# A block-sparse attention with an MLP behind it on one core: the heads of the values are loaded in another order

## The chip, the cores and the metric

The kernel runs on one core of a Trainium2 chip. The metric is the device time of one execution in microseconds (us). Five engines matter, each with its own queue: PE (TensorE, matrix products; its weight loads are listed as PEld), DVE (VectorE), ACT (ScalarE), POOL (GpSimd) and SP (SyncE). POOL and SP issue the transfers (DMAs), which 16 DMA engines carry out.

## The reference

`B, H, S, D = 4, 8, 768, 64`: four batches, eight heads, 768 tokens of 64 values. Attention is restricted to blocks of 32 tokens; its result, with the heads side by side, goes through an MLP with an exact GELU.

```python
scores = scale * np.matmul(q, k.transpose(0, 1, 3, 2))
# mask: neighbouring blocks, first and last block, 3 sampled blocks for each block
scores = np.where(mask, scores, -1000000000.0)
attn = softmax(scores)
x = np.matmul(attn, v)            # (B, H, S, D), then to (B*S, H*D) = (3072, 512)
h = x @ w_in                      # 512 -> 2048
out = gelu(h) @ w_out             # 2048 -> 512
```

## The kernel before

The work is cut into eight units: for each batch a dense one (tokens of three groups of 128, among them the first and the last block, which attend to everything) and one without dense blocks. The attention of unit n+1 runs with the second product of the MLP of unit n (`ffn2_pieces`) as filler between its steps; before it stands the first product of unit n's MLP (`ffn1_step`, L486), eight steps for each unit. The order on every engine is the order in which the program is written; nothing is moved by a scheduler.

Keys and values of a batch lie in one tile, `kvs[b % 2]`, so two batches are held at once. It has 128 partitions, 25 block positions and 388 columns for each: 128 columns of keys, then 260 of values. A head of the values is 24 blocks of 32 tokens with 64 values each. `load_v(b, h)` (L128 to L134) brings one head with one DMA that POOL issues: 32 partitions wide, 24 blocks, 64 values, from float32 in memory to bfloat16 in the tile, that is 768 pieces of 128 bytes written. The 32 partitions are one of four quarters, 0 to 3, and `hh ^= G` chooses it: heads 0 to 7 go to quarters 0, 1, 2, 3, 1, 0, 3, 2. Quarters 0 and 1 are partitions 0 to 63 (the lower half, L), quarters 2 and 3 are partitions 64 to 127 (the upper half, U). Two heads share a quarter's partitions and lie in different columns there, next to a column of ones each.

There are four such sets of eight loads, one for each batch:

- Batch 0, at the start: POOL issues the loads of the keys and queries (L102), the ones (L156), then the eight heads, then the parts of `w_in` (L139). The readers of the tile are the value products of the dense rounds (L400) on PE and POOL's copies of the sampled blocks into `gb` (`gather`, L277), which take all 128 partitions and all value columns.
- Batch 1, during the first product of unit 0's MLP by the program. `turn_keys` and `turn_queries(1)` are issued ahead of it, and `hold_loads` (L150), a tiny copy that reads `qT1`, makes POOL wait until the queries have been turned.
- Batches 2 and 3, each in the first product of an MLP, behind a `hold_loads` on `g`. POOL's copies for the next unit (L277) stand behind them.

The rounds of an attention go through `scores` (L316, PE), `maxima` (L341, L344, DVE), `exponentials` (L358, L362, ACT), `turned` (L375, L380, DVE), `values` (L400 and L436, PE; in pairs of half the heads each), `divided` (L451 to L455, DVE) and `outputs` (L465 on PE, L473 on ACT). `idle_products` (L518) are products without use that fill PE in the first attention.

Of the kernel before, what the change touches and what calls it, by code (L numbers as in the profile page):

```python
# [19 lines left out]
def kernel(  # L20
# [12 lines left out]
    B, H, S, D = q.shape  # L33
# [60 lines left out]
    def sampled(i, r):  # L94
        c0 = GW * (i // 3) + 4 * BW + DW * (i % 3) + BW * r
        return gb[:, c0:c0 + BW]

    def keys(b):
        return kvs[b % 2][:, :, 0:KC]
# [8 lines left out]
    def load_by_token(dst, src, b):  # L108
        rows = by_token(dst).rearrange("p (c h d) -> p c h d", h=H, d=D)
        for c in range(NC):  # L110
            nc.gpsimd.dma_start(out=rows[:, c],
                                in_=src[b, :, P * c:P * c + P].rearrange("h p d -> p h d"))
# [4 lines left out]
    def turn_keys():  # L117
        nc.sync.dma_start_transpose(out=kTd.rearrange("p (n s) -> p n s", s=P), in_=by_token(kn))

    def turn_queries(b):  # L120
        nc.sync.dma_start_transpose(out=qTs[b % 2].rearrange("p c r s -> p (c r) s"), in_=by_token(qn))
# [7 lines left out]
    def load_v(b, h):  # L129
        G, hh = divmod(h, 4)  # L130
        c0 = KC + V2 * G + VW * (hh % 2)
        hh ^= G
        nc.gpsimd.dma_start(out=kvs[b % 2][32 * hh:32 * hh + 32, 0:NB, c0:c0 + D],  # L133
                            in_=v[b, h].rearrange("(n p) d -> p n d", p=BL))  # L134

    def load_w_in(part, n=4):
        w = D_FF // n
        cols = slice(w * part, w * part + w)
        nc.gpsimd.dma_start(  # L139
            out=w_in_sb[:, :, cols], in_=moe_w_in[:, cols].rearrange("(ki p) f -> p ki f", p=P))  # L140
# [7 lines left out]
    def hold_loads(x):  # L148

        nc.gpsimd.tensor_copy(mark, x)  # L150

    def ones(i):
        for hh in range(4):
            for G in range(2):
                c0 = KC + V2 * G + VW * (hh % 2 ^ G) + D
                nc.gpsimd.memset(kvs[i][32 * hh:32 * hh + 32, 0:NB, c0:c0 + 1], 1.0)  # L156
# [18 lines left out]
    load_kq(qn, q, HALVES[0])  # L175
    load_kq(qn, q, HALVES[1])
    ones(0)
    for h in range(H):
        load_v(0, h)


    vf = const.tile([1, NB, NR], I32, name="vf")
# [64 lines left out]
    def gather_fixed(kT, place, copy=None, part=None):  # L247

        copy = copy or nc.vector.tensor_copy
        groups = gb.rearrange("p (g x) -> p g x", x=GW)  # L250
        js = sorted(place)
        runs = [[j for j in js if place[j] - j == c] for c in sorted({place[j] - j for j in js})]
        for run in runs if part != 1 else ():
            i0 = place[run[0]]
            assert i0 % 3 == 0
            for lane in range(min(3, len(run))):
                m, g0 = len(range(lane, len(run), 3)), i0 // 3
                c0, j = BW + KC * lane, run[0] + lane - 1
                copy(
                    groups[:, g0:g0 + m, c0:c0 + 3 * BW].rearrange("p g (w c) -> p g w c", c=BW)[:, :, :, 0:KC],  # L260
                    kT[:, j:j + 3 * m, :].rearrange("p (g w) c -> p g w c", w=3))
        if part == 0:
            return
        at = slice(min(place.values()) // 3, max(place.values()) // 3 + 1)
        n = at.stop - at.start
        copy(groups[:, at, 0:3 * KC].rearrange("p g (l c) -> p g l c", c=KC),
             kT[:, None, 0:1, :].to_broadcast([P, n, 3, KC]))
        copy(  # L268
            groups[:, at, 4 * BW:GW].rearrange("p g (l x) -> p g l x", x=DW)[:, :, :, NR * BW:DW],
            kT[:, None, NB - 1:NB, :].to_broadcast([P, n, 3, KC]))  # L270

    def gather(unit, js, at, c0=0, c1=BW, engine=None):

        src = k0 if (unit.b, c1) == (0, KC) else kvs[unit.b % 2][:, :, c0:c1]
        for j in js:
            for r in range(NR):
                (engine or nc.vector).tensor_copy(sampled(unit.place[j], r)[:, None, c0:c1],  # L277
                                                  src[:, bass.ds(at[j][r], 1), :])
# [105 lines left out]
    def table(func):  # L384

        nc.scalar.activation(junk, zero[0:1, 0:1], func)  # L386
# [94 lines left out]
    def ffn1_step(n, m):  # L481
        T = P * len(units[n].quads)
        hp = psA.tile([P, 2, 512], F32, name="hp", tag="A")
        for i in range(2):
            for ki in range(KIN):
                nc.tensor.matmul(hp[:, i, 0:T], lhsT=w_in_sb[:, ki, (m + i) * P:(m + i + 1) * P],  # L486
                                 rhs=xTs[n % 2][:, ki, 0:T], start=(ki == 0), stop=(ki == KIN - 1))
        for i in ((0, 2),) if m < KOUT - 2 else ((0, 1), (1, 2)):
            nc.scalar.activation(g[:, m + i[0]:m + i[1], 0:T], hp[:, i[0]:i[1], 0:T], AF.Gelu)  # L489
# [13 lines left out]
    def ffn2_pieces(n):  # L503
        for t, quad in enumerate(units[n].quads):
            store_finished()
            op = psO.tile([P, D_MODEL], F32, name="op")
            for m in range(KOUT):
                nc.tensor.matmul(op, lhsT=g[:, m, t * P:(t + 1) * P], rhs=w_out_sb[:, m, :],  # L508
                                 start=(m == 0), stop=(m == KOUT - 1))
                if m == KOUT - 1:  # L510
                    finished.append((n, quad, slice(0, D_MODEL), op))
                yield
# [145 lines left out]
    def more_numbers(js):  # L658
        def load():
            for c in range(0, len(js), 6):  # L660
                known.update(block_numbers(js[c:c + 6], DVE))
        return load
# [5 lines left out]
    def next_keys(b):  # L668
        place_keys(b)
        spare_key(keys(b))  # L670

    for n, unit in enumerate(units):
        nxt = units[n + 1] if n + 1 < len(units) else None
        b = unit.b
        fresh = nxt is not None and nxt.b != b
        if nxt is not None and not fresh:
            if n == 0:
                nc.vector.tensor_copy(kvs[0][:, :, 0:KC], k0)
                more_numbers(J1[6:8])()
            gather_fixed(keys(b), nxt.place)  # L680
            gather(nxt, J1[:8], known)
        for s in range(KOUT // 2):
            ffn1_step(n, 2 * s)
            if s == 0:
                if n == 0:
                    turn_keys()
                    turn_queries(1)
                    gather(nxt, J1[8:], others, engine=nc.gpsimd)
                    ones(1)
                    hold_loads(qT1[0:1, 0:1])  # L690
                    for h in range(H):
                        load_v(1, h)
                elif fresh and b + 2 < B:
                    xT, t0 = column[b, unit.groups[-2][0]]
                    hold_loads(xT[0:1, 0, t0:t0 + 1])
                    load_by_token(qn, q, b + 2)
                    load_by_token(kn, k, b + 2)
                    turn_queries(b + 2)
                elif nxt is not None and not fresh:
                    if b + 1 < B:  # L700
                        turn_keys()
                        hold_loads(g[0:1, 0, 0:1])
                        for h in range(H):
                            load_v(b + 1, h)
                    gather(nxt, J1[8:], others, engine=nc.gpsimd)
            if s == 7 and nxt is not None:
                table(AF.Exp)
                if n > 0 and not fresh and b + 1 < B:
                    next_keys(b + 1)
            if fresh and s == 0:  # L710
                gather_fixed(keys(b + 1), nxt.place)
                gather(nxt, J0[3:9], known)
                gather(nxt, J0[:3], known)
                hold_loads(sampled(nxt.place[J0[2]], NR - 1)[0:1, BW - 1:BW])
                gather(nxt, J0[9:], others, engine=nc.gpsimd)
        filler = ffn2_pieces(n)
        if nxt is None:
            last_output(n)
        elif fresh:
            attention(nxt, filler, [1, 7, 4, 3, 1, 5, 4, 7, 6], (2, 0, 6))  # L720
        elif b + 1 < B:
            attention(nxt, filler, [3, 11, 2, 5, 3, 8, 1, 7, 1], (5,), ahead=units[n + 2],
                      hooks={} if n else {
                          3: [lambda: next_keys(1)], 6: [more_numbers(J0[:3])]})
        else:
            attention(nxt, filler, [7, 6, 3, 5, 3, 8, 7], (1, 0, 5))
# [30 lines left out]
```

## Time and profile before

| | |
|---|---|
| runs of the kernel | 294.49, 298.87 and 293.29 us; median 294.49 us |
| profiled execution, its own time | 296.14 us |
| its span, first to last instruction | 294.4 us |
| mean granted TensorE clock | 0.983 of full |
| busy, share of the span | PE 89%, DVE 73%, ACT 69%, POOL 40% |
| DMAs issued by POOL (q0) | 68352 packets, 13.64 MB |
| instruction queue (q8) | 37 packets, 0.61 MB |
| loads of the values (L133) | 32 DMAs, 0.71 us of POOL's time each in the median |
| from issue to landing of such a load | 3.5 to 13.7 us, median 7.0 us |

The page cuts the span into 40 slices of 7.36 us. These two rows show the share of each slice, in tenths, in which PE was busy, and the clock it was granted:

```profile
PE   1667769978699999999999999999999999999994
...
PEclk9995999999799999999999999999999999999999
```

PE is at 9 tenths nearly everywhere from the twelfth slice on, but at 6 and 7 tenths in the first 50 us, and at 6 in the eleventh slice (74 to 81 us), where the clock was also lower for a part of the slice. The stretches between these times, and the loads in them, are what the change touches.

### The profile page before, as it was taken

Reading aid. Unit: us, or ns where it says so; the run is one execution under the profiler, and the core shown is the slowest. Engines: PE = TensorE matmul, PEld = TensorE weight load, DVE = VectorE, ACT = ScalarE, POOL = GpSimd, SP = SyncE. Lnnn points to the kernel's source line nnn. Section 1 sums busy time; section 2 is a strip of 40 time slices with the busy share of each in tenths; the row PEclk is TensorE's granted clock in tenths of the full one; section 3 lists DMA queues with packets and bytes.
Section 4 is the critical chain, followed back from the end, with each engine's and each line's share of the span. In section 5 each row is a group of like instructions: output and inputs, shape, how many; then the busy total and the mean of one; then the engine's idle time right before and its main releaser. Section 6 shows DMA issues by size and latency. Waiting matters only on the chain.

```text
span 294.4 us, 11255 instructions
## 1 busy us (share of the span) xinstructions
PE 262.4 (89%) x4793; PEld 142.5 (48%) x4793; DVE 213.5 (73%) x477; ACT 204.3 (69%) x374; POOL 118.8 (40%) x219
## 2 busy tenths in 40 slices
PE   1667769978699999999999999999999999999994
PEld 1523445534354455635553555445544555355644
DVE  7595839989697887688997969688948878782000
ACT  8776645686267875698668975796778756976621
POOL 8697999734098000970495005920040014000000
PEclk9995999999799999999999999999999999999999
DMA  6999999999499711991199218991100210021001
GB/s 105 159 86 193 191 166 156 160 172 89 43 115 156 94 73 45 145 72 70 13 154 170 65 40 129 101 61 40 40 0 2 75 39 2 3 74 38 2 36 72
DMA packets 90628, 25.36 MB, mean 86 GB/s; under 512 B 81745, under 2 KB 87634, under 8 KB 90578
## 3 DMA queue, kind: packets, MB, share of 16 engines
q0 software_dynamic: 68352, 13.64, 86.7%
q1 hardware_dynamic: 22226, 11.01, 16.5%
q8 instruction: 37, 0.61, 0.8%
q14 instruction: 13, 0.11, 0.1%
HBM read 27.26 MB, written 6.29 MB: 114 GB/s over the span
## 4 chain that ended last, share of the span: by engine, by line
PE 55%; ACT 17%; DMA 9%; DVE 6%; POOL 6%; issue 4%; POOLq 0%; DVEq 0%; ACTq 0%
PE hp L486 22%; PE op L508 16%; PE av L436 9%; ACT pp L358 8%; DMA kv<-in_v_dram 4%; ACT L386 4%; POOL gb L277 3%; DMA qn<-in_q_dram 3%; ACT g L489 2%; PE sc L316 2%; DVE nm L341 2%; DMA kn<-in_k_dram 2%; PE tx L465 2%; PE av L537 2%; PE op L537 2%
## 5 line engine op out<-in xcount | busy, mean ns | idle before, releaser
L508 PE MATMUL op<-w_out_sb,g 128*128 128x512 bf16 x336 | 87.2, 385 | 0.1
L486 PE MATMUL hp<-xT,w_in_sb 128*128 128x384 bf16 x512 | 85.0, 326 | 0.8 <-ACT xT L473 0.4
L358 ACT ACTIVATE pp<-sc,nm 128x256 bf16<-128x256 f32 x176 | 75.4, 545 | 13.7 <-DVE nm L341 13.5
L489 ACT ACTIVATE g<-hp 128x768 bf16<-128x768 f32 (+1 forms) x72 | 52.1, 738 | 31.4 <-PE hp L486 31.4
L486 PEld LDWEIGHTS <-w_in_sb 128*128 128x128 bf16 x512 | 49.9, 98 | 36.1 <-issue 3.1
L341 DVE TENSOR_REDUCE nm<-sc 128x4 f32<-128x1024 f32 (+1 forms) x48 | 52.9, 1108 | 5.2 <-PE sc L316 5.1
L277 POOL COPY gb<-kv 128x388 bf16 (+1 forms) x87 | 36.9, 475 | 26.4 <-DVE gb L268 24.1
L508 PEld LDWEIGHTS <-g 128*128 128x128 bf16 x336 | 28.8, 98 | 35.4 <-issue 11.9
L277 DVE COPY gb<-kv 128x388 bf16 x177 | 44.2, 329 | 0.5 <-DMA qn<-in_q_dram 0.5
L436 PEld LDWEIGHTS <-pT 64*32 64x32 bf16 (+1 forms) x2400 | 26.3, 92 | 24.0 <-DVE pT L375 10.8
L375 DVE STREAM_TRANSPOSE pT<-pp 128x512 f32<-128x512 f32 (+1 forms) x48 | 31.5, 656 | 4.5 <-ACT pp L358 4.3
L436 PE MATMUL av<-kv,pT 64*32 64x130 bf16 (+1 forms) x1344 | 28.0, 220 | 7.4 <-issue 4.8
L473 ACT COPY xT<-tx 128x512 bf16<-128x512 bf16 (+1 forms) x32 | 13.6, 450 | 20.6 <-PE tx L465 20.6
L316 PE MATMUL sc<-gb,qT 64*32 64x256 bf16 x704 | 19.2, 277 | 8.5 <-ACT pp L358 4.5
L150 POOL COPY mark<-g 1x1 bf16<-1x1 bf16 x2 | 7.0, 3500 | 43.7 <-ACT g L489 43.7
L133 POOL DMA_DIRECT2D kv<-in_v_dram x32 | 22.9, 725 | 1.8 <-DMA qn<-in_q_dram 1.7
L316 PEld LDWEIGHTS <-qT 64*32 64x32 bf16 x832 | 11.6, 90 | 23.8 <-issue 18.0
L362 ACT ACTIVATE pp<-sc,nm 128x768 bf16<-128x768 f32 x16 | 17.1, 1101 | 6.5 <-DVE nm L344 6.5
L344 DVE TENSOR_REDUCE nm<-sc 128x1 f32<-128x768 f32 x16 | 15.0, 945 | 8.4 <-PE sc L316 7.9
L436 PE MATMUL av<-gb,pT 64*32 64x130 bf16 x1056 | 19.9, 222 | 0.0
L386 ACT ACT_TABLE_LOAD x15 | 19.2, 1283 | 0.3
L451 DVE TENSOR_SCALAR den<-av 128x8 f32<-128x8 f32 (+2 forms) x28 | 4.6, 164 | 20.3 <-PE av L436 18.7
(73 smaller groups left out, 244.5 us busy)
## 6 DMA issues: line engine op xcount, KB each, us to landing
out_dram<-os SPq DMA_DIRECT2D x23, 256.0 KB, 2.1
kv<-in_v_dram POOLq DMA_DIRECT2D x32, 96.0 KB, 7.0
kn<-in_k_dram POOLq DMA_DIRECT2D x18, 128.0 KB, 5.4
qn<-in_q_dram POOLq DMA_DIRECT2D x18, 128.0 KB, 5.2
w_in_sb<-in_moe_w_in_dram POOLq DMA_DIRECT2D x4, 512.0 KB, 11.1
w_out_sb<-in_moe_w_out_dram POOLq DMA_DIRECT2D x4, 512.0 KB, 7.9
kn<-in_k_dram POOLq DMA_DIRECT2D x2, 384.0 KB, 5.2
qn<-in_q_dram POOLq DMA_DIRECT2D x2, 384.0 KB, 7.2
```

The lines of the kernel that those rows point to most:

```text
L133: nc.gpsimd.dma_start(out=kvs[b % 2][32 * hh:32 * hh + 32, 0:NB, c0:c0 + D], in_=v[b, h].rearrange("(n p) d -> p n d", p=BL))
L277: (engine or nc.vector).tensor_copy(sampled(unit.place[j], r)[:, None, c0:c1], src[:, bass.ds(at[j][r], 1), :])
L316: nc.tensor.matmul(o, lhsT=qT[rows, j // 4, pr, BL * (j % 4):BL * (j % 4) + BL], rhs=rhs(rows, pr), start=True, stop=True)
L341: nc.vector.tensor_reduce(out=nm[:, 0:2 * n].rearrange("p (g j) -> p g j", g=2), in_=A4[:, :, 0:n, :], op=ALU.max, axis=AX.X, negate=True)
L358: nc.scalar.activation(at[:, x // n, x % n], A[:, a:a + 256].rearrange("p (e c k) -> p e c k", e=2, k=BL), AF.Exp, bias=nm[:, x:x + 1])
L362: nc.scalar.activation(pp[:, 0:S].rearrange("p (c k e) -> p c e k", e=2, k=BL), A[:, 0:S].rearrange("p (c e k) -> p c e k", e=2, k=BL), AF ...
L375: nc.vector.transpose(pt.rearrange("p g c x -> p (g c) x")[:, :, 64 * s:64 * (s + n)].bitcast(F32), pp[:, 0:512 * n].bitcast(F32).rearrang ...
L386: nc.scalar.activation(junk, zero[0:1, 0:1], func)
L436: nc.tensor.matmul(av[32 * s:32 * (s + w), h, V2 * G:V2 * G + V2], lhsT=pv[rows, c % 4, BL * s:BL * (s + w), c // 4], rhs=src[rows], start ...
L486: nc.tensor.matmul(hp[:, i, 0:T], lhsT=w_in_sb[:, ki, (m + i) * P:(m + i + 1) * P], rhs=xTs[n % 2][:, ki, 0:T], start=(ki == 0), stop=(ki ...
L489: nc.scalar.activation(g[:, m + i[0]:m + i[1], 0:T], hp[:, i[0]:i[1], 0:T], AF.Gelu)
L508: nc.tensor.matmul(op, lhsT=g[:, m, t * P:(t + 1) * P], rhs=w_out_sb[:, m, :], start=(m == 0), stop=(m == KOUT - 1))
```

## The change

The eight heads are no longer loaded in the order 0 to 7. A list `VORDER` is made once, when the program is built, and a helper walks through it. The key of the sort is: group of four heads, then the parity of `h % 4 ^ h // 4`, then the head. That gives heads 0, 2, 1, 3, 5, 7, 4, 6, which go to quarters 0, 2, 1, 3, 0, 2, 1, 3: the halves are L, U, L, U, L, U, L, U where they were L, L, U, U, L, L, U, U. All four sets are changed. The number of the loads, their sizes, and where in POOL's queue the sets stand are the same.

```diff
+    VORDER = sorted(range(H), key=lambda h: (h // 4, (h % 4 ^ h // 4) % 2, h % 4))
+
+    def load_values(b):
+        for h in VORDER:
+            load_v(b, h)
+
...
     ones(0)
-    for h in range(H):
-        load_v(0, h)
+    load_values(0)
...
                     hold_loads(qT1[0:1, 0:1])
-                    for h in range(H):
-                        load_v(1, h)
+                    load_values(1)
...
                         hold_loads(g[0:1, 0, 0:1])
-                        for h in range(H):
-                            load_v(b + 1, h)
+                        load_values(b + 1)
                     gather(nxt, J1[8:], others, engine=nc.gpsimd)
```

## The prediction, as it was put on record before the run

> **What bounds the kernel now.** I began with the chain of waits that ended last. Most of it is work on PE, which a load of the values cannot touch. Two stretches of it are no PE work at all:
>
> ```profile
> 13.00 12.37 DMA kv<-in_v_dram
> ...
> 76.16 1.20 issue
> 77.36 1.29 PE av L436 x80
> ```
>
> (Start, length, what.) From 13.00 to 25.37 the kernel waits for the last of the eight loads of batch 0. The gap ahead of 77.36 looks unrelated. The timeline of PE prices both:
>
> ```profile
> 25.51 1.47 PE L400 MATMUL av<-kv,ptd 64*64 64x130 bf16 x45 [1.58 <-DMA kv<-in_v_dram]
> ...
> 77.36 0.40 PE L436 MATMUL av<-kv,pT 64*32 64x130 bf16 x20 [2.34 <-issue]
> ```
>
> Three products of L400 ran at 23.61; the fourth reads heads 6 and 7 and waited 1.58 us. POOL's first copy waited 1.90 us for the same landing. The second gap is 2.34 us with the operands ready. In the trace's list of packets, one of the instruction queue's 37 packets (0.61 MB, so about 16 KB each) starts at 74.97 and takes 0.99 us, and PE goes on 1.4 us after its end. Two gaps in the first attention look the same: packets ending at 36.45 and 41.36, PE going on at 37.88 and 42.71. So PE had run out of instructions. These packets come about every 127 pairs of weight load and product (the 15th after 1903 pairs); the one at 74.97 was due after some 1016 pairs, which PE reached at 70.8. It came 4.2 us late, and in these 4.2 us the DMA engines were full of the values of batch 1. [...]
>
> Next, how fast these loads go. Stretches of the trace, the last two figures being the mean number of packets that each DMA engine has under way and GB/s:
>
> ```profile
> 48.50:49.50 1.00, 1.00 (x8) 0.59 (x6) 0.98 (x1) 0.72 (x1) 1.00 (x2) 1.00 2.50 154
> 65.50:66.50 1.00, 1.00 (x23) 0.33 (x7) 0.98 (x2) 1.00 (x4) 1.00 (x2) 1.00 2.11 130
> 69.50:70.50 1.00, 0.04 (x2) 0.04 (x4) 1.00 (x3) 0.28 (x1) 0.00 (x1) 1.00 4.92 56
> 70.50:71.50 1.00, 1.00 (x60) 0.61 (x60) 1.00 (x2) 0.43 (x2) 0.00 (x0) 1.00 4.24 109
> ```
>
> The first is the load of the keys by token: packets of 128 bytes too, but over all 128 partitions, at a steady 154 GB/s. The others are the values of batch 1, 32 partitions each. They start as fast, then packets pile up (5 under way instead of 2.5) and the rate swings between 56 and 109. The landings of the second, third and fourth of the eight say where it swings (issue, and time to landing):
>
> ```profile
> L133 POOL DMA_DIRECT2D kv<-in_v_dram x1: 713/713/713, 64.4 to 64.4; - x1
> ...
> DMA to landing us min/median/max: 5.9/5.9/5.9
> L133 POOL DMA_DIRECT2D kv<-in_v_dram x1: 709/709/709, 65.1 to 65.1; - x1
> ...
> DMA to landing us min/median/max: 5.9/5.9/5.9
> L133 POOL DMA_DIRECT2D kv<-in_v_dram x1: 709/709/709, 65.8 to 65.8; - x1
> ...
> DMA to landing us min/median/max: 6.9/6.9/6.9
> ```
>
> Read in the same way, the eight land at 68.6, 70.3, 71.0, 72.7, 73.5, 75.2, 75.9 and 76.8. A load whose predecessor went to the same half lands 1.7 us after it; one whose predecessor went to the other half, 0.7 to 0.8 us after it (the last of all, with nothing behind it, 0.9). So a half takes in about one load per 1.7 us, and where the halves change, two loads go in side by side. [...]
>
> **The change part by part.** It adds and removes no instruction: eight issues of 0.71 us per set stay on POOL, in the same places, so what stands behind them (the parts of `w_in`, POOL's copies L277, the next `hold_loads`) is issued as before. No wait is added. A reader needing all eight waits for the last, whichever head that is; of the L400 products the fourth still needs head 6, now the last, and the three ahead of it gain or lose nothing that the fourth doesn't hold back.
>
> *Speed of a set.* With L and U in turn, each half gets a load every 1.7 us, one set of four beside the other: from the first landing at 68.6, the last L at 68.6 + 3 x 1.7 = 73.7 and the last U half a step later, 74.5 instead of 76.8. That is 2.2 us sooner. Bounds: 0, if the loads still go one by one; 2.9 us, if each lands 0.75 us after the one before (76.8 - 68.6 - 7 x 0.75). I take 2.2, which the half's own rate sets. Below nothing is a rival below.
>
> *Batch 0.* The eight land at 14.1, 16.2, 17.6, 19.1, 20.9, 22.1, 24.2 and 25.4. This is less regular: by the trace's semaphore events 12 of the 16 engines finished the last load by 22.4, and the slowest at 25.4; an instruction packet that took 2.43 us at 15.22 falls among them. If that engine keeps its lag, the last landing is at 25.4 - 2.2 = 23.2. PE is through with its third product at 23.9 and POOL with its own issues at 23.6, so both waits go whole, and no more: PE gains 1.6 us (its 1.58), POOL 1.9. What is late next is the round itself: ACT waited 2.6 us for the maxima and these 2.1 us for PE's scores, which stand behind the L400 products in PE's queue, so they move with it. POOL's copies for the second and third group end at 35.3 and 39.2, ahead of the products that read them (38.05 and 42.7), and move as far. I put **-1.6 us**; bounds 0 and -1.9.
>
> *Batch 1.* If the DMA engines are through 2.2 us sooner, the instruction packet starts at 72.8 and PE may go on at 72.8 + 0.99 + 1.4 = 75.2. PE wants it at 74.78 + 0.24 = 75.0. The gap of 2.34 us shrinks to 0.2: **-2.2 us**, on the path, as DVE waits for just these products (2.58 us ahead of the division at 78.73) and the MLP's next step for its result. What is late next there is the dense round's transpose on DVE (its exponentials end at 76.5), which is read later. Bounds 0 and -2.3.
>
> *Batches 2 and 3.* Issued at 120.8 and 183.4, landed within 7.7 us of each issue, during products of the MLP, and no instruction packet starts inside (121.41 and 133.46, 182.75 and 195.65 stand around them). The view of L133 lists nobody who waited. Cost 0; the cover is the first product, 10.5 us, and the rounds up to the next unit's copies.
>
> Sum: 1.6 + 2.2 = 3.8 us. Against the profiled execution: 296.14 - 3.8 = 292.3. That run was 1.65 us above the median of the three runs; against the median: 294.49 - 3.8 = **290.7 us**, or 1.3%.
>
> **The rivals.**
>
> *The clock comes along.* Three stretches:
>
> ```profile
> 23.30:26.70 3.40, 1.82 (x50) 1.35 (x48) 1.76 (x2) 3.03 (x8) 1.50 (x5) 0.51 1.25 200
> ...
> 74.50:77.90 3.40, 1.06 (x65) 0.64 (x66) 1.36 (x2) 1.10 (x1) 0.00 (x0) 1.00 0.33 61
> 78.00:81.30 3.30, 3.30 (x51) 1.70 (x35) 2.50 (x7) 0.58 (x1) 0.91 (x2) 0.50 0.02 5
> ```
>
> The first figure after the length is PE's busy time, the third from the end the granted clock. Both waits lie in the first two rows, PE little busy in them, and the 3.4 us that follow ran at half clock, with PE busy all the time. If the filled stretches keep the clock, up to half of 3.4 us is saved after each, and where other engines take part in the pace perhaps 1.2 us (an estimate from these rows): 290.7 - 2.4 = 288.3. The stretch from 23.3 is at half clock already, which speaks against the first of the two.
>
> *Nothing overlaps.* All 16 engines serve every load in order; the side-by-side landing might need two full loads of one half ahead of it, some engines running ahead while others lag. Then the mean pace of a set stays at (76.8 - 68.6) / 7 = 1.2 us and the time at 294.5. The irregular landings of batch 0 speak for it, the regular ones of batch 1 against. [...]
>
> *Slower: a change of the half is what costs.* The rate falls to 56 in stretches that begin soon after packets of a new half start (69.5 above). If the change itself brings the slow stretch, there are seven in place of three; by the packets' starts a load with it takes 1.6 us and one without 0.9, so a set is 4 x 0.7 = 2.8 us longer. Batch 0 then holds PE and POOL 2.8 us more, and the instruction packet starts 2.8 us later: 294.5 + 5.6 = 300.1. It decides from the point where landings after a change come more than 1.2 us apart; in batch 1 they came 0.7 to 0.8 us apart, against it.
>
> **How the numbers follow.** Forecast (290.7, or up to 293 if only one of the two terms comes) 0.56; the clock with it 0.17; nothing overlaps 0.20; slower 0.07. The first three reach from 288.3 to 294.5; with half a microsecond for the spread of the runs the range is 287.8 to 295.0. Two per cent, about what a measurement of this kernel can tell from no change, is 5.9 us: 288.6 and 300.4. Faster than that are most of the clock's cases and a few of the forecast's, 0.19; slower is about half of the last rival, 0.04; the rest, 0.77, lies between.
>
> **What would show it.** In the changed profile: landings of batch 1 about 0.85 us apart throughout, the last some 10.8 us after the first issue instead of 13.1; a rate that stays near 100 GB/s or above; PE's waits of 1.58 and 2.34 us nearly gone. If the sets are quicker but the 2.34 us stay, the instruction packet waits for something else. If the landings alternate as before or come 1.2 us apart, the forecast is wrong at its first step.

## The result, and the profile after

| | before | after |
|---|---|---|
| median of 22 runs each, on one chip | 294.89 us | 292.25 us |
| lowest and highest | 293.29, 298.87 | 290.35, 294.87 |
| ratio, with its 95% interval | | 0.9905 (0.9884 to 0.9927) |
| profiled execution, its span | 296.14, 294.4 us | 292.31, 290.5 us |
| mean granted clock in it | 0.983 | 0.994 |

The change made the kernel 0.95% faster, 2.8 us of 294.89. Single executions of one kernel scatter by 2 to 3%, so a ratio leaves out those over 1.5% above the fastest of their kernel, and where only six were run the median stands beside it and nothing is ranked by them.

Lines behind the added helper are six further down: L400, L436 and L486 are now L406, L442 and L492. The page's rows of slices, the changed kernel:

```profile
PE   1757669988698899989998999989988999899995
...
PEclk9999979999999999999999999999999999999999
```

The fourth slice (22 to 29 us) was at half clock before and is not now; the low slice of the clock is the sixth (36 to 44 us). The eleventh (73 to 80 us) still has PE at 6 tenths, now at full clock. In the chain of waits no load of the values is left. Its first long "issue" stretches stand in the first attention:

```profile
38.00 2.44 issue
40.44 1.60 PE av L442 x73
```

The timeline of PE (start, length, line, operation, count; in brackets the wait ahead and what ended it):

```profile
22.90 0.88 PE L406 MATMUL av<-kv,ptd 64*64 64x130 bf16 x48
...
34.52 0.37 PE L442 MATMUL av<-kv,pT 64*32 64x130 bf16 x24 [1.39 <-issue]
...
40.44 0.30 PE L442 MATMUL av<-kv,pT 64*32 64x130 bf16 x5 [2.44 <-issue]
...
74.91 0.40 PE L442 MATMUL av<-kv,pT 64*32 64x130 bf16 x20 [2.36 <-issue]
```

The wait of 1.58 us for batch 0 is gone: all 48 products run at once at 22.90. The wait of 2.34 us in the second attention is not: it is 2.36 us, and begins earlier. So one of the two terms of the forecast came.

What the loads did. The third load of batch 1, and the rate while the set ran (as before, the last two figures are the packets under way for each DMA engine and GB/s):

```profile
64.50:65.50 1.00, 0.84 (x53) 0.64 (x29) 1.00 (x4) 0.76 (x2) 1.00 (x2) 1.00 2.44 140
66.50:67.50 1.00, 0.36 (x2) 0.00 (x0) 0.96 (x3) 0.58 (x1) 0.00 (x0) 1.00 5.44 61
68.50:69.50 1.00, 1.00 (x50) 0.56 (x28) 0.95 (x3) 0.90 (x2) 0.00 (x0) 1.00 4.47 56
71.50:72.50 1.00, 1.00 (x9) 0.30 (x6) 1.00 (x3) 0.00 (x0) 0.00 (x0) 1.00 2.13 222
```

```profile
L133 POOL DMA_DIRECT2D kv<-in_v_dram x1: 729/729/729, 61.9 to 61.9; - x1
...
DMA to landing us min/median/max: 7.3/7.3/7.3
```

The eight land at 64.3, 67.8, 69.3, 70.8, 71.8, 72.6, 72.8 and 73.3. The pairs of before are gone, but the loads do not land 0.85 us apart: the middle ones come 1.5 us apart and the packets pile up as before (5.44 under way, 56 to 61 GB/s). What is left over at the end is less, and the last four follow within 2.5 us.

A set is best measured from its first packet to its last landing, both from the trace:

| set, us | batch 0 | batch 1 | batch 2 | batch 3 |
|---|---|---|---|---|
| before, L L U U L L U U | 14.13 | 11.55 | 11.01 | 11.23 |
| after, L U L U L U L U | 10.90 | 11.34 | 10.34 | 10.09 |

Where the time went, as milestones. "Gap ends" is where PE goes on in the second attention, "next" the first product of the MLP behind it (the three middle rows are from the experiments below, the last column is worked out):

| profiled execution | halves in batch 0 | division that ends the first attention | first product of unit 0's MLP | gap ends | next | gap end to next |
|---|---|---|---|---|---|---|
| before | L L U U | 43.68 | 45.61 | 77.36 | 82.23 | 4.87 |
| only batch 1 alternating | L L U U | 42.42 | 44.35 | 76.53 | 81.30 | 4.77 |
| only batches 2 and 3 alternating | L L U U | 42.23 | 44.15 | 76.05 | 80.82 | 4.77 |
| only batch 0 alternating | L U L U | 42.04 | 44.75 | 75.69 | 78.93 | 3.24 |
| after | L U L U | 42.09 | 44.48 | 74.91 | 78.16 | 3.25 |

From 82.23 and 78.16 on the two kernels go step by step alike (32.69 and 32.70, 29.88 and 29.88, 32.71 and 32.71 us, and so on; only the last, 29.22 and 29.49, differs by more than 0.04): all that is gained, 4.07 us in these two executions, is gained in the first 82 us.

The pair is not the whole picture. In the first attention the executions with the old order differ from each other as much as from the new one: the first product of unit 0's MLP comes at 44.15 and 44.35 in two of them, earlier than in either row with the new order. What these rows do share is the stretch behind it, up to "next": 36.6 to 37.0 us with the old order in batch 0, 33.7 and 34.2 with the new.

The last column goes with the clock. Stretches of PE with the granted clock as the third figure from the end, first before, then after:

```profile
74.60:78.00 3.40, 1.06 (x73) 0.74 (x76) 1.26 (x2) 1.10 (x1) 0.00 (x0) 1.00 0.28 56
78.00:81.40 3.40, 3.40 (x51) 1.70 (x35) 2.60 (x7) 0.58 (x1) 1.00 (x2) 0.50 0.02 5
```

```profile
70.70:74.10 3.40, 1.69 (x14) 0.70 (x11) 2.65 (x5) 1.75 (x2) 0.00 (x0) 1.00 1.64 116
74.10:77.50 3.40, 2.43 (x99) 1.77 (x101) 1.31 (x4) 0.58 (x1) 0.25 (x1) 1.00 0.02 5
```

All stretches of half clock in these traces, but for those that the end cuts off, are 3.4 us long or twice that, and within one execution their starts lie whole multiples of 3.41 us apart (23.38 and 78.00 before, 16 of them). I laid the rows on that grid. Before, the whole gap falls into one cell (PE busy 1.06 us of 3.40), and the next cell runs at half clock. After, a gap of the same length is split over two cells (1.69 and 2.43 us busy), and the clock stays. The grid lies differently in each execution (a stretch of half clock starts at 39.97 after the change and at 40.55 in only0 below, in the same place of the program), so where the gap falls on it is in part chance.

### The profile page after: what moved, and what is told of

It is laid out like the page before. It is cut to its first block, busy times and chain, and to the rows that moved or that the text cites. A ratio compares the mean times of both kernels' runs of the same rounds, so it can differ in the third digit from the quotient of the medians.

```text
span 290.5 us, 11198 instructions
## 1 busy us (share of the span) xinstructions
PE 251.4 (87%) x4736; PEld 141.5 (49%) x4793; DVE 213.1 (73%) x477; ACT 204.1 (70%) x374; POOL 117.1 (40%) x219
## 3 DMA queue, kind: packets, MB, share of 16 engines
q1 hardware_dynamic: 22226, 11.01, 16.6%
## 4 chain that ended last, share of the span: by engine, by line
PE 63%; ACT 19%; DVE 8%; issue 5%; DMA 3%; POOL 1%; DVEq 0%; POOLq 0%; ACTq 0%
PE hp L492 26%; PE op L514 14%; PE av L442 11%; ACT pp L364 8%; ACT L392 4%; PE sc L322 3%; ACT g L495 3%; DMA qn<-in_q_dram 3%; PE tx L471 2%; PE av L543 2%; PE op L543 2%; DVE nm L347 2%; DVE nm L350 2%; ACT pp L368 1%; PE op L524 1%
## 5 line engine op out<-in xcount | busy, mean ns | idle before, releaser
L492 PE MATMUL hp<-xT,w_in_sb 128*128 128x384 bf16 x512 | 85.0, 326 | 0.8 <-ACT xT L479 0.4
L514 PE MATMUL op<-w_out_sb,g 128*128 128x512 bf16 x288 | 75.8, 380 | 5.0 <-issue 4.0
L492 PEld LDWEIGHTS <-w_in_sb 128*128 128x128 bf16 x512 | 50.0, 98 | 36.0 <-issue 3.1
L514 PEld LDWEIGHTS <-g 128*128 128x128 bf16 x336 | 28.5, 97 | 35.1 <-issue 11.2
L283 DVE COPY gb<-kv 128x388 bf16 x177 | 43.4, 324 | 0.5 <-DMA qn<-in_q_dram 0.5
L442 PEld LDWEIGHTS <-pT 64*32 64x32 bf16 (+1 forms) x2400 | 26.7, 92 | 26.2 <-DVE pT L381 11.1
L442 PE MATMUL av<-kv,pT 64*32 64x130 bf16 (+1 forms) x1344 | 28.7, 222 | 9.4 <-issue 6.6
L133 POOL DMA_DIRECT2D kv<-in_v_dram x32 | 25.0, 793 | 1.7 <-DMA qn<-in_q_dram 1.1
L322 PEld LDWEIGHTS <-qT 64*32 64x32 bf16 x832 | 11.5, 90 | 22.6 <-issue 16.6
L157 POOL COPY mark<-g 1x1 bf16<-1x1 bf16 x2 | 3.8, 1888 | 42.2 <-ACT g L495 42.2
L442 PE MATMUL av<-gb,pT 64*32 64x130 bf16 x1056 | 20.2, 223 | 0.0
```

Source lines behind the costliest of these rows:

```text
L322: nc.tensor.matmul(o, lhsT=qT[rows, j // 4, pr, BL * (j % 4):BL * (j % 4) + BL], rhs=rhs(rows, pr), start=True, stop=True)
L442: nc.tensor.matmul(av[32 * s:32 * (s + w), h, V2 * G:V2 * G + V2], lhsT=pv[rows, c % 4, BL * s:BL * (s + w), c // 4], rhs=src[rows], start ...
```

## The experiments

**Which set carries it** (labels only0, only1, only23). The alternating order is kept in one place, the others go back to heads 0 to 7.

```diff
-        for h in VORDER:
+        for h in (VORDER if b == 0 else range(H)):   # b == 1, b > 1 in the others
```

> The alternating order in batch 0 alone. Theory 1 (the whole gain starts with the last landing of batch 0, which came 3.3 us earlier with the change): -1.6 to -2.6 us against the kernel before, most of the change's -0.95%; the last landing of batch 0 near 22.1 us, the batch 1 loads in the old order and PE's gap behind them in the second attention still about 2.3 us. Theory 2 (the terms of the prediction: 1.6 us from batch 0 and the rest from batch 1): about -1.6 us, with the rest missing.

> The alternating order in batch 1 alone. Theory 1 (batch 0 carries all; in batch 1 the set is only about 0.2 to 0.7 us shorter and the instruction packet stays as late): within 0.5 us of the kernel before, PE's gap in the second attention still about 2.3 us. Theory 2 (the prediction: the instruction packet comes 2.2 us sooner): -1 to -2 us, gap under 1.5 us.

> The alternating order in batches 2 and 3 alone. Both theories: the sets are about 0.7 to 1.1 us shorter (11.0 and 11.2 us from first packet to last landing before, 10.3 and 10.1 with the change), nobody waits for them, the time is that of the kernel before within 0.5 us. A rival (they hold up instruction packets or stores of the output in the later attentions): -0.5 us or more.

| | median, us | ratio to before, 95% |
|---|---|---|
| only0 | 293.24 | 0.9916 (0.9877 to 0.9956) |
| only1 | 295.74 | 0.9974 (0.9938 to 1.0010) |
| only23 | 296.59 | 0.9985 (0.9943 to 1.0026) |

The kernel before stood at 295.9 us on this chip. Batch 0 carries the gain nearly alone; of the other two no gain is shown. The profiled executions of only1 and only23 (299.2 and 298.42 us) lost 3.8 us later on, in their third step; the last section tells of it, and the rows used here stand ahead of it. The timeline of PE of only0, and then of only1, at the gap:

```profile
75.69 0.40 PE L442 MATMUL av<-kv,pT 64*32 64x130 bf16 x20 [2.69 <-issue]
```

```profile
23.94 0.84 PE L406 MATMUL av<-kv,ptd 64*64 64x130 bf16 x45 [0.68 <-DMA kv<-in_v_dram]
...
76.53 0.40 PE L442 MATMUL av<-kv,pT 64*32 64x130 bf16 x20 [2.77 <-issue]
```

The gap is there with either order in batch 1, although the set of batch 1 took 9.93 us in only1 and 11.82 in only0. The second fence prices batch 0 again: with the old order PE went on at 23.94 here (23.89 in only23), where the execution shown before the change had 25.51. The 1.58 us were a late case: the wait was 0.68 and 0.42 us here, and PE's scores ahead of it had started 0.5 to 0.6 us later in that execution already (22.43 against 21.80 to 21.91).

The profiles of the runs below share the program up to the end of the first attention, so the order in batch 0 can be compared over more than one pair (pool_late and fours, which differ there, are left out):

| batch 0 | profiles | last landing of the set | first product of unit 0's MLP | end of DVE's copies behind it |
|---|---|---|---|---|
| L L U U | before, only1, only23, both_old | 23.1 to 25.4, mean 24.0 | 43.9 to 45.6, mean 44.5 | 56.4 to 58.5, mean 57.3 |
| L U L U | after, only0, no_v1, paced1, nohold1, late_v1, hold_turn, both | 22.1 to 22.6, mean 22.3 | 43.1 to 45.0, mean 43.8 | 55.6 to 57.5, mean 56.4 |

The values always land earlier with the new order. What PE and DVE make of it is 0.7 and 0.9 us on the mean, with ranges that overlap.

**What if the halves change least** (label fours). The same loads in two blocks of four: L L L L U U U U.

```diff
+    FOURS = (0, 1, 5, 4, 2, 3, 7, 6)
+
-        for h in VORDER:
+        for h in FOURS:
```

> Four heads of the lower half, then four of the upper, in all batches (one change of the half where the kernel before has three and the changed one seven). Theory of the prediction (two loads go in side by side at each change, a half by itself takes 1.7 us a load): sets longer than before, 12.5 to 13 us in batches 2 and 3 against 11.0 to 11.2, and the kernel slower by 1 to 2 us. Rival (a set runs at full speed until a half is choked, after about 2.4 loads when they go to one half and 3.5 when they alternate, and from then on each change of the half brings a slow stretch): sets of 10 to 11.5 us, no slower than before, with a steady rate once choked and one slow stretch at the change.

It was slower: 300.27 us, ratio 1.0138 (1.0094 to 1.0182). PE's timeline:

```profile
25.02 0.84 PE L408 MATMUL av<-kv,ptd 64*64 64x130 bf16 x45 [1.77 <-DMA kv<-in_v_dram]
...
79.86 0.61 PE L444 MATMUL av<-kv,pT 64*32 64x130 bf16 x20 [4.83 <-issue]
```

Both waits are there and the second is twice as long. In the sets of batches 2 and 3, which nothing else disturbs much, the order of the halves has a clear dose: 12.4 us with one change (12.40 and 12.37), 11.0 to 11.2 with three (before), 10.1 to 10.3 with seven (after). Over all profiles, but for four sets of batch 2 that the last section tells of, it is 10.9 to 11.9 with three and 9.8 to 10.6 with seven. That a change of the half is what costs, the rival on the slower side, is refuted. The order alone is worth about 18% of a set from end to end, 8% for this change.

**Is it POOL's chain, or PE's instructions?** (labels pool_late, no_v1, paced1, nohold1). pool_late holds POOL back by four fills of a scratch tile (3.15 us) ahead of its first copies from the values; no_v1 leaves out the eight loads of batch 1, whose values stay zero; paced1 puts a fill behind each of these loads; nohold1 lets them go without waiting for the turned queries.

```diff
+            for _ in range(4 if t == 0 else 0):    # pool_late
+                nc.gpsimd.memset(pad, 0.0)
...
-        for h in VORDER:                           # no_v1
+        for h in VORDER if b != 1 else ():
...
+            if b == 1:                             # paced1, behind each load
+                nc.gpsimd.memset(pad, 0.0)
...
-                    hold_loads(qT1[0:1, 0:1])      # nohold1
```

> The changed kernel, but POOL fills a scratch tile four times (some 2.5 us) ahead of its first copies of sampled values, so that POOL starts them as late as in the kernel before, while the loads land as early as with the change. Theory 1 (PE's first wait carries the gain of batch 0; POOL has slack): as the changed kernel, 0.99 of the kernel before. Theory 2 (POOL's chain of copies and issues carries it): the gain is gone, 0.997 to 1.005.

> The changed kernel without the eight loads of the values of batch 1 (batch 1 is computed with zeros in their place). Theory 1 (the gap of 2.3 us in PE in the second attention is an instruction packet that waits behind these loads): the gap is under 0.5 us, the packet near 70 us, and the kernel is 2 to 4 us faster than the changed one: 0.977 to 0.984 of the kernel before. Theory 2 (the packet is late for another reason, such as the weights, the keys or PE's own pace): gap still near 2.3 us, 0.99 of the kernel before.

> The changed kernel with POOL filling a scratch tile (some 0.7 us) behind each load of batch 1, so that the loads come 1.4 us apart, about as fast as they are taken in. Theory 1 (a backlog of issued loads holds the instruction packet up): little backlog, the packet comes 2 to 4 us sooner, the gap in the second attention falls under 1 us: 0.980 to 0.987 of the kernel before; the set from first packet to last landing is not longer than 12 us. Theory 2 (any load under way holds it up, with or without backlog): gap near 2.3 us, 0.99 of the kernel before or worse, as POOL's filling may stop DVE.

> The changed kernel without the hold ahead of the loads of batch 1, so that POOL issues them about 5 us sooner, while the keys and queries of batch 1 are being turned. Theory 1 (the instruction packet waits for the end of this set): the set ends ahead of 70 us, the gap shrinks by 2 us: 0.980 to 0.987 of the kernel before. Theory 2 (the turning of keys and queries shares the DMA engines and comes later by as much): the products of the next unit wait for the turned keys, 0.99 to 1.005.

On this chip the kernel before stood at 295.65 us.

no_v1: median of six 290.31 us, ratio 0.9788 (0.9734 to 0.9843). The products that stood still at the gap run through, 24 of them without a break:

```profile
73.30 0.42 PE L442 MATMUL av<-kv,pT 64*32 64x130 bf16 x24
```

The eighth instruction packet starts 0.49 us after it is due here (counted as in the prediction, by weight loads), against 4.15 us before and 4.08 us after the change. So it is shown that this packet is late because the values of batch 1 are being loaded, as the prediction had it. (late_v1, below, shows the same with the loads moved instead of left out.)

pool_late: median of six 292.31 us, ratio 0.9801 (0.9744 to 0.9858). Its POOL timeline shows the delay in place:

```profile
25.17 3.15 POOL L655 MEMSET pad<- 128x768 bf16 x4
28.27 3.85 POOL L284 COPY gb<-kv 128x260 bf16 x11
```

POOL's first copies start at 28.27, later than before the change (25.52), and yet the kernel is no slower than the changed one. It still doesn't settle whether POOL's earlier start carries a part of the gain. In its profile the first attention ends as late as before the change (division at 43.38, first product at 45.30, DVE's copies through at 59.05), and it was late ahead of the fills already (the last load of batch 0 issued at 14.55 instead of 12.34). The time came back later: the values of batch 1 now go out at 68.9 instead of 60.5 us, and the gap shrinks to 0.97 us. A loss and a gain are mixed.

paced1: 295.87 us, ratio 1.0008 (0.9977 to 1.0038). Meant to keep the packets from piling up, it failed as a test. Its DVE timeline:

```profile
64.06 5.39 DVE L126 TENSOR_SCALAR kv<-ptd 128x768 bf16<-128x768 bf16 x4
```

After the change the same four operations take 1.43 us. PE waited 5.97 us for what DVE does behind them, which covers anything at the instruction packet.

nohold1: 297.11 us in the median of six, above the kernel before. Its set of batch 1 took 14.10 us, over the turning of the keys that the wait had kept it behind. The wait is likely worth having; its profiled execution lost time in the third step too, as in only1.

**The values of batch 1 out of the way** (label late_v1), and a try against the scatter (label hold_turn). late_v1 loads them behind the placing of batch 1's keys, after the products that stand at the gap. In hold_turn the values of batches 2 and 3 wait for the turned keys, and POOL's copies go ahead of them.

```diff
+    def values_behind_keys():                      # late_v1
+        hold_loads(keys(1)[0:1, NB, 0:1])
+        load_values(1)
...
-                    hold_loads(qT1[0:1, 0:1])
-                    load_values(1)
...
-                          3: [lambda: next_keys(1)], 6: [more_numbers(J0[:3])]})
+                          3: [lambda: next_keys(1), values_behind_keys], 6: [more_numbers(J0[:3])]})
```

```diff
                         turn_keys()                # hold_turn
-                        hold_loads(g[0:1, 0, 0:1])
-                        load_values(b + 1)
-                    gather(nxt, J1[8:], others, engine=nc.gpsimd)
+                    gather(nxt, J1[8:], others, engine=nc.gpsimd)
+                    if b + 1 < B:
+                        hold_loads(kTd[0:1, 0:1])
+                        load_values(b + 1)
```

> The changed kernel, with the eight loads of batch 1 issued behind the placing of batch 1's keys (a hold on the last of them in the second attention), some 8 us later than now. Theory 1 (the instruction packet due near 68 us waits behind these loads): that packet starts within 1 us of the moment it is due, PE's gap of 2.3 us there shrinks under 1 us and no stretch of half clock follows it: 0.975 to 0.983 of the kernel before. Theory 2 (only their order matters): 0.99, gap as before. If the loads now end too late, the copies for the next unit wait for them and the second step (32.7 us between first products) grows.

> The changed kernel, with the loads of batches 2 and 3 behind the copies of POOL and behind the landing of the turned keys, in place of the hold on g. Theory 1 (in some executions POOL's hold ends 3 us sooner, the loads run into the turning of the keys, and a unit takes 33.7 in place of 29.9 us; that makes much of the scatter between runs): every such step is 29.9 us, the runs scatter over less than 3 us, 0.983 to 0.990. Theory 2 (the scatter has another cause): median and scatter as the changed kernel, 0.99; if the later loads hold anybody up, more.

late_v1 had a median of 292.44 us from six against 296.3 on its chip, ratio 0.9868 (0.9802 to 0.9935). The gap is gone and the next unit's first product starts at 75.09 instead of 78.16. PE's timeline at that place:

```profile
71.84 0.40 PE L442 MATMUL av<-kv,pT 64*32 64x130 bf16 x20 [0.21 <-issue]
```

None of the 3 us reached the end in the profiled execution (a span of 291.1 us against 290.5): its third step took 33.38 us where after the change it takes 29.88 (more on that in the last section). The interval overlaps that of the change itself, so that it beats the changed kernel is not shown.

hold_turn: 296.36 us, ratio 1.0001 (0.9955 to 1.0046), the gain of the change lost. Its third and fifth steps took 31.0 and 33.4 us. Its profile holds one thing more. Up to the second attention its program is that of the changed kernel, the values of batch 1 are loaded at the same place (61.28 to 73.19 us), and yet there is no gap. DVE's copies ended 1.1 us later and a stretch of half clock ran from 62.0 to 65.4, so PE needed the eighth instruction packet only at 70.50, where the changed kernel needed it at 68.39, and the packet started at 71.20. PE was through with these products no later than after the change, so the gap is slack that a later PE uses up.

**The order alone, with the values of batch 1 out of the way** (labels both, both_old). Both edits together, in the alternating and in the old order of heads; the one line between them:

```diff
-        for h in VORDER:                           # both
+        for h in range(H):                         # both_old
```

> Both edits together, heads in the alternating order. Theory 1: the gains add, 0.970 to 0.980. Theory 2 (they are one gain, seen from two sides): as the better of the two alone.

> Both edits, heads in the old order 0 to 7. Theory 1 (what the order is worth is PE's first wait in batch 0, 1.0 to 1.6 us, and the later stall of the second attention is another matter): 1 to 1.6 us slower than the same edits with the alternating order, PE's first value products wait for the loads again. Theory 2 (the order was worth something only through the second attention, where the loads are out of the way now): within 0.5 us of the alternating order.

both: 293.39 us, 0.9934 (0.9896 to 0.9971). both_old: 296.23 us, 1.0028 (0.9986 to 1.0070). The gains do not add up to the 0.970 to 0.980 of the first theory for both: it is no better than late_v1 alone, and its fifth step took 33.4 us as in hold_turn. Between the two orders, the intervals don't meet and the medians lie 2.84 us apart. The size is less sure than that: the plain averages of the executions that the ratio keeps are 293.5 us for both (eleven of twelve) and 294.3 for both_old (six of twelve), 0.9 us apart. PE's timeline of both_old has no gap left to shrink:

```profile
72.64 0.40 PE L442 MATMUL av<-kv,pT 64*32 64x130 bf16 x20 [0.19 <-issue]
```

Nor is there a half-clock stretch behind it. So the order is likely worth something without the gap and without the clock lost behind it; how much, between 0.9 and 2.8 us, is open. Where it lies in both_old I can't show: its profiled execution was its quickest (292.07 us, 4.2 below its median). PE's first products from the values wait for no load there (48 run at once at 23.01), which the first theory had expected them to.

## Why the prediction was right, and where it was wrong

The forecast was 290.7 us, 3.8 us down; measured were 292.25 us and about 2.6 us down from the medians. The sign, and that a faster batch 0 frees the start, were right. Of its two terms one was sized after an unusually late execution and the other did not come; a part of the time came from a rival instead. The branch "up to 293 if only one of the two terms comes" is what happened. That the time fell 0.7 us below it came from outside the sum, the clock among it, and for the number that is luck.

*What bounds the kernel: right.* no_v1 shows that the gap is an instruction packet that waits behind the values of batch 1, and only0 that the landing of batch 0 costs time at the end.

*Speed of a set, taken at -2.2 us: right in kind, mis-sized.* The landings come in turn and the dose of the halves is there, but the sets of batches 2 and 3 got 0.7 and 1.1 us shorter, and batch 1 only 0.2 in the execution shown (1.6 in only1). The step that failed was to read 1.7 us as the rate of one half with the other beside it for free. In the trace's packets the middle of an alternating set takes 1.45 to 1.5 us a load; before, a pair took 2.45 us, which is 1.2 a load. In the steady state seven changes are no quicker than three, and by the prediction's own sign (landings 0.85 us apart, wrong if 1.2) its first step failed in batch 1. What differs is how long the first loads run at full rate (1.44 loads a us in the best half us before, 1.47 after): about three and a half loads instead of two and a half until the packets pile up. Why, the traces don't show.

*Batch 0, -1.6 us: the size was right against the profiled execution, too large against the median.* The division that ends the first attention came 1.59 us earlier (43.68 to 42.09). By the landing the set shrank by 3.2 us, by the point at which 12 of the 16 engines were through only by 0.9: the slowest engine lost its lag of 3 us, which the prediction had let it keep. But the wait of 1.58 us belongs to that execution; in two other profiles of the old order PE went on at 23.9, 1.0 us after the 22.9 of the changed kernel, and in both_old there was no wait at all. Over the profiles compared above the first attention ends 0.7 us earlier on the mean.

A part was then given back. The first product came only 1.13 us earlier: ahead of it PE's waits for instructions grew from 1.14 and 1.34 us to 1.39 and 2.44, and a stretch of half clock from 40.0 to 43.4 fell on the end of the attention. DVE, which had its division early, went on to its copies. Its timeline, before and after:

```profile
43.68 0.16 DVE L451 TENSOR_SCALAR den<-av 96x8 f32<-96x8 f32 x1 [2.83 <-PE av L436]
...
50.35 8.11 DVE L277 COPY gb<-kv 128x388 bf16 x24
```

```profile
42.09 0.16 DVE L457 TENSOR_SCALAR den<-av 96x8 f32<-96x8 f32 x1 [4.61 <-PE av L442]
...
48.43 7.74 DVE L283 COPY gb<-kv 128x388 bf16 x24
```

The copies end 2.30 us earlier (58.46 and 56.16), as they also ran a little quicker, and the second attention starts from them. Measured from the first product they end 12.85 us behind it before and 11.68 after. That is not the order's doing as far as the profiles go: the other six of the changed order have 12.3 to 14.2 (only0 alone has 11.63), the other three of the old order 12.5 to 12.9. After the change and in only0 it is the first product that came late, held up by the half clock.

*Batch 1, -2.2 us at the gap: wrong, 0 came.* The step that failed is "if the DMA engines are through 2.2 us sooner, the instruction packet starts at 72.8" with PE wanting it at 75.0 as before. The packet did start at 72.47, but not because the set was quicker: it started 9.8 us behind the set's first packet before and 10.5 after, and 9.9 and 10.0 us behind it in only0 and only1, whose sets took 11.82 and 9.93 us. It came earlier because the set began earlier: the values of batch 1 were issued at 60.53 instead of 63.73, as POOL waits there for queries that were turned earlier. And PE wanted the packet 2.47 us earlier too (68.39 instead of 70.86). Its lateness stayed at 4.1 us. So both halves of the step were wrong: the packet's start does not follow the length of the set, and the prediction had moved the one end of the wait and left the other in place, although its own batch 0 term said that PE would come 1.6 us earlier. Its sign for this case, "the instruction packet waits for something else", was wrong as well: no_v1 shows that it waits for these values.

*The clock comes along: partly true.* It was given 0.17. At the second place it came: from the end of the gap to the next product 4.87, 4.77 and 4.77 us in the old order of batch 0, 3.24 and 3.25 in the new, so 1.5 to 1.6 us, where the rival put 1.2. It came without the gap being filled, by where the gap falls on the grid. Over the runs it is less: from each run's mean clock and span, (1 - clock) x span / 1.71 gives the number of half-clock stretches, on the mean 2.41 before and 1.86 in only0 on the same chip. At 0.8 us for each (the slope of time on that number over the runs of before) or 1.6 (this place), 0.54 fewer are worth 0.4 to 0.9 us. The means differ by 2.45 us (296.03 and 293.58), so about two thirds or more is not clock. Of that rest the earlier end of the first attention and of DVE's copies shows 0.7 to 0.9 us on the mean of the profiles. The remaining 0.6 us or more has no place that these runs show.

*Nothing overlaps:* refuted by fours and by the sets of batches 0, 2 and 3; in batch 1 of the execution shown the landings did come at about its pace (64.29 to 73.30, 1.3 us a load). *Batches 2 and 3, cost 0:* right; only23 has no gain that can be told. One reading there was off: the instruction packet at 195.65 lies inside batch 3's set, whose last load landed at 196.14.

## What to carry to other kernels

Where a train of transfers each fills one quarter of the partitions, alternate the halves: it added no instruction here, and the order was worth up to 2 us of 12 in a set (12.4 in fours, 10.1 to 10.3 after). When a step moves earlier, move both ends of every later wait before counting it as shortened: a wait whose two ends hang on the same step does not shrink. And take a wait from more than one profile before putting it into a sum: 1.58 us in one execution were 0.68, 0.42 and nothing in three others.

## What was not expected of the hardware

*A grid for the clock.* A gap of about 2.4 us in PE's work cost nothing or 1.6 us more, with its place against a 3.41 us grid (the four rows above). Laid on such a grid, all fourteen profiles agree on when the clock dropped: from 16 us on, each of the 27 cells at full clock with PE busy for less than 1.45 us was followed by half clock (1.06 us from 74.60 before, 1.44 from 36.56 after), and no cell with 1.82 us or more was. Between these two figures it went either way: 1.69 us from 19.97 before was followed by half clock, 1.67 from 19.49 after was not.

*Fills on POOL and DVE's key placing.* With fills of 128x768 between the loads (paced1), DVE's four operations took 5.39 us instead of 1.43. That the fills hold DVE up is the likely reading; no run separates it from the loads beside them. In the trace of before, DVE's copies (L277) are slower beside POOL's small fills too: five of them fill the 1.44 us from 55.35, while POOL writes the ones (L156), and ten the 1.55 us from 56.85, with POOL idle.

*A hold of two lengths.* The 1x1 copy that holds the loads of batch 2 back took 3.51 us in some executions and 0.27 in others. POOL's row and the keys' placing on DVE, after, and then only1:

```profile
113.31 3.51 POOL L157 COPY mark<-g 1x1 bf16<-1x1 bf16 x1 [21.03 <-ACT g L495]
```

```profile
119.41 2.47 DVE L125 TENSOR_SCALAR kv<-ptd 128x768 bf16<-128x768 bf16 x4 [2.64 <-DMA ptd<-kn]
```

```profile
116.31 0.27 POOL L157 COPY mark<-g 1x1 bf16<-1x1 bf16 x1 [22.37 <-ACT g L495]
```

```profile
126.08 1.54 DVE L125 TENSOR_SCALAR kv<-ptd 128x768 bf16<-128x768 bf16 x4 [4.78 <-DMA ptd<-kn]
```

With the short one the values go out 3 us earlier, into the turning of the keys; DVE waits about 5 us for it and the third step takes 33.4 to 33.7 us instead of 29.9. All four profiles with the short hold show it (only1, only23, nohold1, late_v1), and none of the seven with the long one (the other three profiles have another hold there). It accounts for some of the scatter between executions. What decides the length is open, and hold_turn, meant to take it away, did not help. The same copy ahead of batch 3 took 0.27 us in five of the eleven profiles, after the change among them, and there it cost nothing (a fifth step of 29.9 us).
